# Chunked attention with a gated convolution: the first half pair in two halves, fp32 value products for part of the first group, a new order and new buffers

## Chip, cores and metric

The kernel runs on one core of a Trainium2 chip. The metric is device time in microseconds (us). Before the change the median of three runs is 286.18 us (285.96 to 287.81).

## The reference, cut to what matters

Shapes: batch 8, heads 8, sequence 576, head size 64; model width 512; chunks of 64 tokens; everything fp32.

```python
# attention inside each chunk of 64 tokens
scores = scale * np.matmul(q_c, k_c.transpose(0, 1, 2, 4, 3))      # scale = 1/8
scores = scores - np.max(scores, axis=-1, keepdims=True)
attn = np.exp(scores)
attn = attn / (np.sum(attn, axis=-1, keepdims=True) + 1e-09)
out = np.matmul(attn, v_c)
x = out.transpose(0, 2, 1, 3).reshape(B, S, 512)
# gated convolution
for k in range(5):                                                 # causal, per channel
    gate_pre += conv_w[k][None, None, :] * xp[:, k:k + S, :]
gate = 1.0 / (1.0 + np.exp(-gate_pre))
val = x @ w_val
return (gate * val @ w_out)
```

The weights arrive as 64-bit words and are turned into fp32 on the chip.

## The kernel before

**Tiling.** The 8 x 576 tokens are cut into 9 groups g of 512 tokens. In a group the heads come in two pairs of loads, p = 0 and 1 (each holds four heads of 64 channels, as two blocks of 128 channels), and the width of 512 is four blocks c or m of 128. A dense product of fp32 accuracy is made of three fp32r products: high part times high part, low weights times high x, high weights times low x; so weights and x are split into two fp32r parts.

**Pieces.** The whole program is a string of small pieces with their indices, `ORDER`; a loop at the end of the kernel (L516 on) calls one function per piece. Instructions of an engine run in the order of that string, and each engine's queue is in order. The buffers of each kind are numbered, and `SLOTS` says which number each new tile gets, in the order of the pieces; `HOME` says which kinds share buffers.

- Loads on the SyncE queue (SP): `lk`, `lq`, `lv` bring k, q, v of a pair, 512 KB each; `lw` a block of weights, 512 KB; `lc` the conv taps.
- Scores: `S g p b` is half b of a pair, 16 fp32 products of 64x64x64 on quarters of the array (32 for both halves); both halves lie in the one tile s of PSUM. `mx` (VectorE, DVE) takes the maximum, `sb` (DVE) subtracts it into an e_row buffer in SBUF, `ex` (ScalarE, ACT) takes exponentials, `sm` (DVE) sums and inverts, `nm` normalises on GpSimd (POOL) or DVE (`nmD`). Pair 0 1 has a way of its own: `mh`, `ml` split the maximum, `sp` subtracts it by four TensorE (PE) products, `ep` is the exponential from PSUM. Pairs 3 0, 4 0, 7 0, 8 0 have another: `ng`, `ea` (sixteen exponentials on ACT that also sum), `rc`.
- `T g p` transposes in eight products into the one tile et of PSUM, `ec` copies it out, `A g p` is attention times V (32 products of 64x64x64) into two PSUM tiles, u = 0 and 1.
- `xc g p u` copies x for the convolution, `xr` rounds it to its high part, `xd` makes the low part, `hl` fills the halo.
- `k0` and `k` are the conv taps, `sg` the sigmoid; `V g m c` the three value products, `vc` their eviction from PSUM to SBUF, `gs`/`gm` gate times value, `gr`, `gd` the split of that; `P g t c` the three output products, `oc` the eviction, `st` the store.
- `w1` to `w7`, `wb` turn a block of weights into fp32 (kept in `wq`) and split it into `v_hi`, `v_lo` or `o_hi`, `o_lo`.
- `W n` is n dummy bf16 products.

Products, attention times V and dummies share four PSUM buffers of one bank each, named ps. A last letter on a piece names its engine: G is GpSimd, D VectorE. All recorded instructions have the line of the helper `run`, L160, so rows are told apart by the names of their tiles (t is any buffer of the kind t2 or t4, ld any load, acc the raw weights or the conv sums).

The set `BY_HALF` is empty before; functions with an optional b work on half b of a pair when it is given.

Of the kernel before, what the change touches and what calls it, by code (L numbers as in the profile page):

```python
# [93 lines left out]

SLOTS = dict(
    ld="054321504315240135240512054310305213053400533503052304",
    ps="0000312130130213012310321023021303210321320123102031013202012013201231021301032103120302310310132013"
       "120312012032",
    acc="03210321023012302130123012",
    s="000000000000000000",  # L100
# [7 lines left out]
    mh="0",  # L108
# [12 lines left out]
def chunk_attention_gated_conv(ctx, tc, q, k, v, w_val, conv_w, w_out, out):  # L121
# [65 lines left out]
    def begin(g):  # L187
        return parts(g)[0][0]
# [383 lines left out]
```

## Time and profile before

| | |
|---|---|
| median of three runs | 286.18 us |
| profiled execution, its span | 286.4 us |
| TensorE busy | 274.4 us (96%), 3344 instructions |
| VectorE busy | 245.8 us (86%), 357 |
| ScalarE busy | 198.1 us (69%), 451 |
| GpSimd busy | 105.2 us (37%), 93 |
| DMA | 42.47 MB, mean 148 GB/s |
| chain that ended last | PE 69%, DVE 19%, DMA 3%, issue 3% |

The span goes from the first to the last instruction of the profiled execution. A busy TensorE is not TensorE at its peak: a product's record (some 0.40 us) overlaps the next one's, so prices are read as differences of starting times. Idle time of an engine that is not the bottleneck costs nothing by itself.

### The profile page before, as it was taken

The page shows a single profiled execution, that of the slowest core. Times are in us where ns is not written, and L with a number is a line of the kernel's source. Part 1 is how long each engine was busy: PE and PEld are TensorE (multiplying, and loading weights), DVE is VectorE, ACT ScalarE, POOL GpSimd, SP SyncE. Part 2 cuts the span into 40 slices and gives each one's busy share as a digit, 9 for nine tenths or more (in the row PEclk, how much of TensorE's full clock was granted, in tenths as well). Part 3 has the DMA queues.
Part 4 walks back from the last instruction along what each step waited for, and adds up shares of the span by engine and source line. Part 5 has one row for each costly group of instructions (what it writes and reads, how often), then busy time and mean ns, then how long its engine had stood idle before and what let it go on. Part 6 is the DMA issues. An engine that isn't in the chain of part 4 may idle for free.

```text
span 286.4 us, 7971 instructions
## 1 busy us (share of the span) xinstructions
PE 274.4 (96%) x3344; PEld 217.3 (76%) x3347; DVE 245.8 (86%) x357; ACT 198.1 (69%) x451; POOL 105.2 (37%) x93
## 2 busy tenths in 40 slices
PE   7978899999999999999999999989999999999994
PEld 3456688878888887878787888767678778888883
DVE  0899779999999999999999999999999899974210
ACT  2479588898999979964898696788586742751101
POOL 1457775273013506551874003976400400013100
PEclk9999799999999999999999999999999999999999
DMA  7999964457002605666250256441100121021245
GB/s 280 416 391 359 380 239 130 169 181 260 3 2 78 222 0 185 221 223 211 86 185 2 73 201 218 173 144 44 39 0 1 39 89 61 0 100 49 110 171 195
DMA packets 14291, 42.47 MB, mean 148 GB/s; under 512 B 1712, under 2 KB 1712, under 8 KB 14256
## 3 DMA queue, kind: packets, MB, share of 16 engines
q1 hardware_dynamic: 14256, 41.97, 40.9%
q8 instruction: 26, 0.43, 0.6%
q14 instruction: 9, 0.07, 0.1%
HBM read 32.53 MB, written 9.44 MB: 147 GB/s over the span
## 4 chain that ended last, share of the span: by engine, by line
PE 69%; DVE 19%; DMA 3%; issue 3%; POOL 2%; ACT 2%; SPq 0%; POOLq 0%
PE ps L160 61%; DVE acc L160 8%; PE s L160 5%; DVE t L160 4%; PE et L160 4%; DVE rs L160 3%; DMA ld<-in_v 2%; DMA ld<-in_q 1%; POOL acc L160 1%; POOL t L160 1%; DVE mx L160 1%; ACT x L160 1%; DVE t2o L160 1%; DVE t4a L160 0%; DVE x L160 0%
## 5 line engine op out<-in xcount | busy, mean ns | idle before, releaser
L160 DVE SCALAR_TENSOR_TENSOR acc<-x,cw,acc 128x516 f32<-128x516 f32 (+1 forms) x144 | 105.1, 771 | 0.9 <-POOL acc L160 0.6
L160 PE MATMUL ps<-t,v_hi 128*128 128x512 f32 x240 | 85.3, 402 | 0.0
L160 PE MATMUL ps<-t,v_lo 128*128 128x512 f32 x136 | 53.9, 396 | 0.0
L160 PEld LDWEIGHTS ps<-t,v_hi 128*128 128x128 f32 x240 | 45.2, 188 | 11.0 <-issue 0.5
L160 PE MATMUL ps<-o_hi,t 128*128 128x512 f32 x120 | 46.4, 403 | 0.8 <-ACT x L160 0.7
L160 PE MATMUL ps<-o_lo,t 128*128 128x512 f32 x76 | 30.0, 395 | 0.0
L160 DVE TENSOR_REDUCE mx<-s 128x16 f32<-128x1024 f32 x18 | 21.8, 1211 | 9.3 <-PE s L160 9.2
L160 PEld LDWEIGHTS ps<-t,v_lo 128*128 128x128 f32 x136 | 25.7, 189 | 5.1
L160 PEld LDWEIGHTS ps<-o_hi,t 128*128 128x128 f32 x120 | 22.5, 188 | 7.3 <-ACT x L160 1.1
L160 POOL TENSOR_TENSOR t<-e_row,rs 128x1024 f32<-128x1024 f32 x13 | 26.4, 2033 | 4.2 <-DVE rs L160 3.4
L160 PEld LDWEIGHTS s<-ld,ld 64*64 64x64 f32 x1152 | 19.4, 139 | 9.6 <-issue 7.7
L160 ACT CAST t<-ps 128x512 fp32r<-128x512 f32 x34 | 19.4, 596 | 10.0 <-PE ps L160 8.1
L160 PE MATMUL s<-ld,ld 64*64 64x64 f32 x1152 | 22.0, 227 | 2.9 <-issue 1.9
L160 ACT ACTIVATE e_row<-s,mx 128x64 f32<-128x64 f32 x64 | 19.0, 352 | 4.7 <-DVE mx L160 4.7
L160 POOL COPY x<-x 128x16 f32<-128x16 f32 x8 | 2.8, 354 | 52.6 <-DVE acc L160 44.9
L160 PEld LDWEIGHTS ps<-t,ld 64*64 64x64 f32 x960 | 16.3, 140 | 5.0 <-issue 2.1
L160 PE MATMUL ps<-t,ld 64*64 64x64 f32 x960 | 18.1, 225 | 1.9 <-DVE t2i L160 1.1
L160 POOL TENSOR_SCALAR acc<-x,cw 128x516 f32<-128x516 f32 (+1 forms) x7 | 12.7, 1820 | 19.2 <-ACT x L160 7.4
L160 ACT ACTIVATE acc<-x,cw 128x516 f32<-128x516 f32 (+1 forms) x24 | 17.6, 740 | 1.9 <-DVE x L160 1.8
L160 ACT ACT_TABLE_LOAD x14 | 18.0, 1283 | 0.9 <-PEq L561 0.7
L160 DVE TENSOR_REDUCE rs<-e_row 128x16 f32<-128x1040 f32 x14 | 17.2, 1228 | 1.6 <-ACT e_row L160 1.6
L160 ACT COPY x<-ps 128x512 f32<-128x512 f32 (+3 forms) x38 | 16.0, 476 | 3.3 <-issue 2.0
(302 smaller groups left out, 572.5 us busy)
## 6 DMA issues: line engine op xcount, KB each, us to landing
ld<-in_k SPq DMA_DIRECT2D x18, 512.0 KB, 5.8
ld<-in_q SPq DMA_DIRECT2D x18, 512.0 KB, 5.9
ld<-in_v SPq DMA_DIRECT2D x18, 512.0 KB, 5.0
out<-t SPq DMA_DIRECT2D x10, 256.0 KB, 2.3
acc<-in_moe_w_val SPq DMA_DIRECT2D x4, 512.0 KB, 7.5
acc<-in_moe_w_out SPq DMA_DIRECT2D x4, 512.0 KB, 7.1
out<-t2j SPq DMA_DIRECT2D x3, 256.0 KB, 2.5
out<-t2b SPq DMA_DIRECT2D x3, 256.0 KB, 3.1
```

What stands on the lines that cost most here:

```text
L160: return tc.keep_in_program_order(fn(*args, **kwargs))
```

## The change

**What it does.** Pair 0 0 is worked in halves: each half of its scores has a PSUM tile of its own (s and et), and `mx`, `sb`, `ex`, `sm`, `nm`, `T`, `ec` and `A` are called for each half, while the loads stay whole. In group 0, for channel blocks c = 0 and 1 (pair 0), a new piece `F g m c` makes the value product as one fp32 product from the fp32 weights in `wq` and the x of the convolution; the eight products of `F` stand for 24 of `V`, and `xr 0 0`, `xd 0 0` are gone. The order of all pieces and all buffer numbers are new, with some pieces on other engines. `ea` is written as four calls of `ey`, with the same sixteen exponentials.

```diff
-ORDER = """zw,lk 0 0,zi,lq 0 0,W 8,lw v 2,lw v 0,lq 0 1,zr 1,zm,lk 0 1,lw v 1,zr 0,lv 0 0,lq 1 0,S 0 0 0,S 0 0 1,W 15,mx 0 0,
+ORDER = """zw,zi,zr 0,zr 1,lk 0 0,lq 0 0,W 2,zm,W 1,W 2,lw v 3,lw v 2,w1G v 2,w5 v 2,S 0 0 0,lw v 0,mx 0 0 0,sb 0 0 0,S 0 0 1,
...
-BY_HALF = set()
+BY_HALF = {(0, 0)}
...
     def sc(g, p, b):
-        if b == 0:
-            s_ps[g, p] = tile_of("s", [P, 2, 2, 4, D], F32, banks)
-        at = s_ps[g, p]
-        if b == 1 and (g, p) in BY_HALF:
-            at = s_ps[g, p, 1] = tile_of("et", [P, 2, 2, 4, D], F32, banks)
+        alone = (g, p) in BY_HALF
+        if b == 0 or alone:
+            s_ps[g, p, b] = tile_of("et" if b else "s", [P, 2, 2, 4, D], F32, banks)
+        at = s_ps[g, p, b if alone else 0]
...
-    def sm(g, p):
+    def sm(g, p, b=None):
-        rss[g, p] = r = tile_of("rs", [P, 16], F32)
-        run(V.tensor_reduce, out=r, in_=probs[g, p], op=ALU.add, axis=AX.X)
+        if (g, p) not in rss:
+            rss[g, p] = tile_of("rs", [P, 16], F32)
+        r, e = rss[g, p], probs[g, p]
+        if b is not None:
+            r, e = r.rearrange("p (h b c) -> p h b c", h=2, b=2)[:, :, b], half_rows(e, b)
+        run(V.tensor_reduce, out=r, in_=e, op=ALU.add, axis=AX.X)
         run(V.reciprocal, out=r, in_=r)
...
-    def tr(g, p):
-        et_ps[g, p] = tile_of("et", [P, 8, P], F32, banks)
+    def tr(g, p, b=None):
+        if (g, p) not in et_ps:
+            et_ps[g, p] = tile_of("et", [P, 8, P], F32, banks)
         for j in range(8):
-            run(E.transpose, out=et_ps[g, p][:, j, :], in_=normed[g, p][:, 2 * j:2 * j + 2, :].rearrange("p b k -> p (b k)"), identity=ident)
+            if b is not None and j // 2 % 2 != b:
+                continue
+            at = j if b is None else 4 * b + 2 * (j // 4) + j % 2
+            run(E.transpose, out=et_ps[g, p][:, at, :], in_=normed[g, p][:, 2 * j:2 * j + 2, :].rearrange("p b k -> p (b k)"), identity=ident)
...
+    def vf(g, m, c):
+        if c == 0:
+            v_ps[g, m] = tile_of("ps", [P, T], F32, banks)
+        run(E.matmul, v_ps[g, m], lhsT=wq["v", c].bitcast(F32)[:, m * P:(m + 1) * P], rhs=xs[g][:, c, begin(g):],
+            start=c == 0, stop=c == NH - 1)
...
-                  S=sc, mx=mx, sb=sb, ex=ex, sm=sm, ng=ng, ea=ea, rc=rc, nm=nm, T=tr, ec=ec, A=av, hl=hl, xc=xc, xr=xr, xd=xd, k0=k0,
+                  S=sc, mx=mx, sb=sb, ex=ex, sm=sm, ng=ng, ea=ea, ey=ey, rc=rc, nm=nm, T=tr, ec=ec, A=av, hl=hl, xc=xc, xr=xr, xd=xd, k0=k0,
```

**What moves, on TensorE.** The first value products of group 0. Before, on TensorE, the transposes of pair 0 1 (et_356) and the score piece of pair 1 1 (s_369) stand ahead of the first group of three fp32r products (t_348 is the rounded x, t4a its low part):

```order
L160 MATMUL et_356<-ident,t_339 128x128 x8
L160 MATMUL s_369<-ld_161,ld_226 64x64 x32
L160 MATMUL ps_410<-t_348,v_hi 128x512
L160 MATMUL ps_410<-t_348,v_lo 128x512
L160 MATMUL ps_410<-t4a,v_hi 128x512
```

After, the score piece of pair 1 0 is followed by single products of x_224 (the x of the convolution) with t_154 and t_246 (the fp32 weights of blocks 0 and 1), and transposes stand between them:

```order
L160 MATMUL s_312<-ld_307,ld_309 64x64 x32
L160 MATMUL ps_351<-x_224,t_154 128x512
L160 MATMUL et_358<-ident,t_356 128x128 x8
L160 MATMUL ps_351<-x_224,t_246 128x512
L160 MATMUL ps_393<-x_224,t_154 128x512
```

One product of x and a weight block now stands where three stood, and the casts of x are not ahead of it.

**What moves, on ScalarE, in the start.** Before, from the split of the maximum of pair 0 1 (mh) to the first copies of x (e_row_65<-s is `ep`, t4b<-et is `ec 0 0`, t_348<-ps is `xr 0 0`):

```order
L160 CAST mh_236<-mx_228 128x16
L160 ACTIVATE t2n<-acc_99 128x512
L160 ACTIVATE t2o<-t2o 128x512
L160 ACTIVATE e_row_65<-s_183 128x16x64
L160 COPY t4b<-et_250 128x1024
L160 CAST v_hi<-t2q 128x512
L160 CAST t_348<-ps_300 128x2x256
L160 COPY x_163<-ps_301 128x2x256
L160 CAST t_348<-ps_301 128x2x256
```

After, from the same mh to the second copy of x (ps_255 and ps_256 are the results of `A 0 0`):

```order
L160 CAST mh_217<-mx_215 128x16
L160 CAST v_hi<-t_154 128x512
L160 COPY t_234<-et_226 128x2x256 x2
L160 ACTIVATE t_244<-t_244 128x512
L160 ACTIVATE e_row_65<-s_179 128x16x64
L160 CAST v_hi<-t_231 128x512
L160 CAST v_hi<-t_246 128x512
L160 COPY x_224<-ps_255 128x2x256
L160 ACTIVATE t2a<-acc_242 128x512
L160 COPY x_224<-ps_256 128x2x256
```

Three roundings of weights (v_hi) stand there where one stood, the copies of the two halves of `ec 0 0` (t_234) come ahead of `ep` and not behind it, and the two casts of x are gone.

**What moves, on ScalarE, ahead of the first sixteen exponentials.** Before, between the copy `ec 1 1` and the group `ea 3 0` (the last row):

```order
L160 COPY t_726<-et_707 128x1024
L160 ACTIVATE e_row_65<-e_row_65 128x16x64
L160 ACTIVATE t2b<-t2b 128x512
L160 CAST t_821<-ps_771 128x2x256
L160 COPY t2j<-ps_666 128x512
L160 CAST t_821<-ps_772 128x2x256
L160 COPY x_618<-ps_772 128x2x256
L160 COPY x_618<-ps_771 128x2x64
L160 COPY x_618<-ps_771 128x2x192
L160 COPY t2d<-ps_700 128x512
L160 COPY t_857<-et_812 128x1024
L160 ACTIVATE e_row_64,rs_871<-s_734,mx_837 128x64 x16
```

After, from the exponential `ex 2 1` to the same group:

```order
L160 ACTIVATE e_row_65<-e_row_65 128x16x64
L160 COPY t2q<-ps_351 128x512
L160 COPY x_514<-ps_768 128x2x64
L160 COPY x_514<-ps_768 128x2x192
L160 CAST t_817<-ps_769 128x2x256
L160 COPY x_514<-ps_769 128x2x256
L160 CAST t_817<-ps_768 128x2x256
L160 ACTIVATE t2o<-t2o 128x512
L160 ACTIVATE acc_840<-x_514,cw 128x516
L160 ACTIVATE acc_842<-x_514,cw 128x516
L160 COPY t_862<-et_804 128x1024
L160 ACTIVATE e_row_64,rs_900<-s_733,mx_834 128x64 x16
```

One eviction of value products (t2q) stands there where two stood (t2j, t2d), two conv starts (acc) stand between the casts of x and the last copy of transposes, and the group follows that copy in both.

## Rows read from the trace of the kernel before

**Rows 1.** Table of stages; columns as in its first line, counts in parentheses.

```profile
core 0: us, PE busy (x) PEld busy (x) DVE busy (x) ACT busy (x) POOL busy (x), PEclk, DMA share, GB/s
...
23.10:34.69 11.59, 9.62 (x225) 7.20 (x215) 10.39 (x17) 8.28 (x16) 7.71 (x6) 0.85 0.99 364
...
62.00:136.00 74.00, 73.17 (x986) 59.75 (x985) 71.82 (x106) 63.16 (x136) 27.00 (x21) 1.00 0.43 146
136.00:204.00 68.00, 66.14 (x894) 53.10 (x893) 66.51 (x90) 55.57 (x128) 36.66 (x28) 1.00 0.36 119
...
sum 286.40, PE 274.43 PEld 217.33 DVE 245.78 ACT 198.05 POOL 105.18; mean PE 30.49 PEld 24.15 DVE 27.31 ACT 22.01 POOL 11.69
```

**Rows 2.** Timeline of PE: start, duration, tiles, count; waits and their releasers in brackets.

```profile
64.68 1.16 PE L160 MATMUL ps<-t,ld 64*64 64x64 f32 x64 [0.83 <-DMA ld<-in_v]
...
190.06 1.16 PE L160 MATMUL ps<-t,ld 64*64 64x64 f32 x62 [1.07 <-DVE t2i L160]
...
203.97 0.50 PE L160 MATMUL ps<-o_hi,t 128*128 128x512 f32 x1 [0.67 <-ACT x L160]
```

**Rows 3.** Table of stages, columns as in rows 1, the stretch at a lower clock.

```profile
31.06:34.47 3.41, 3.41 (x63) 2.55 (x65) 3.41 (x6) 0.81 (x2) 1.66 (x2) 0.50 1.01 359
```

**Rows 4.** Timeline of PE: score pieces and the first value product.

```profile
12.29 1.16 PE L160 MATMUL s<-ld,ld 64*64 64x64 f32 x64
...
23.18 0.50 PE L160 MATMUL ps<-t,v_hi 128*128 128x512 f32 x1
...
29.76 0.81 PE L160 MATMUL s<-ld,ld 64*64 64x64 f32 x40 [1.94 <-issue]
```

**Rows 5.** Timeline of PE without pauses: score, attention times V, transposes.

```profile
37.67 1.16 PE L160 MATMUL s<-ld,ld 64*64 64x64 f32 x64
38.76 0.50 PE L160 MATMUL ps<-t,v_hi 128*128 128x512 f32 x1
...
45.70 1.11 PE L160 MATMUL ps<-t,ld 64*64 64x64 f32 x64
46.74 1.10 PE L160 MATMUL et<-ident,t 128*128 128x128 f32 x8
47.59 0.48 PE L160 MATMUL ps<-t,v_hi 128*128 128x512 f32 x1
```

**Rows 6.** Timeline of PE: the last five products, first and last.

```profile
281.46 0.40 PE L160 MATMUL ps<-o_lo,t2a 128*128 128x512 f32 x1
...
282.39 0.39 PE L160 MATMUL ps<-o_hi,t2h 128*128 128x512 f32 x1
```

**Rows 7.** Timeline of POOL: the third and the fourth load arrive.

```profile
7.18 0.63 POOL L160 TENSOR_SCALAR t<-acc 128x512 f32<-128x512 f32 x1 [5.79 <-DMA acc<-in_moe_w_val]
...
8.52 0.64 POOL L160 TENSOR_SCALAR t2s<-acc 128x512 f32<-128x512 f32 x1 [0.65 <-DMA acc<-in_moe_w_val]
```

**Rows 8.** Groups by line and form, 5 to 45 us: busy, mean ns.

```profile
L160 DVE TENSOR_REDUCE mx<-s 128x16 f32<-128x1024 f32 x6 | 7.3, 1214 | 9.3 <-PE s L160 9.2
...
L160 ACT COPY x<-ps 128x512 f32<-128x512 f32 x5 | 2.8, 590 | 0.0
...
L160 ACT ACTIVATE e_row<-s 128x1024 f32<-128x1024 f32 x1 | 1.0, 1026 | 0.1
...
L160 DVE TENSOR_TENSOR t4b<-ps,t 128x512 fp32r<-128x512 f32 x2 | 1.3, 674 | 0.0
...
L160 DVE SCALAR_TENSOR_TENSOR t2r<-t,t2r 128x512 uint32<-128x512 uint32 x1 | 0.7, 683 | 0.0
```

**Rows 9.** Timeline of ACT: first exponential of ea 3 0, eviction after it.

```profile
51.81 0.32 ACT L160 ACTIVATE e_row<-s,mx 128x64 f32<-128x64 f32 x1 [0.93 <-DVE mx L160]
...
56.57 0.67 ACT L160 COPY t2i<-ps 128x512 f32<-128x512 f32 x1
```

**Rows 10.** Table of stages, columns as in rows 1, ten microseconds of the middle.

```profile
80.00:90.00 10.00, 10.00 (x107) 8.10 (x106) 9.93 (x18) 9.97 (x40) 0.54 (x1) 1.00 0.01 2
```

**Rows 11.** Groups by line and form, whole span: a DVE step beside POOL.

```profile
L160 DVE TENSOR_TENSOR t2o<-t,t2n 128x512 fp32r<-128x512 f32 x1 | 2.1, 2135 | 0.0
```

More of the change, by code (lines that the diff above doesn't have):

```diff
@@ L293, in mx @@
         if b is None:
-            run(V.tensor_reduce, out=mxs[g, p], in_=flat(s_ps[g, p]), op=ALU.max, axis=AX.X)
+            run(V.tensor_reduce, out=mxs[g, p], in_=flat(s_ps[g, p, 0]), op=ALU.max, axis=AX.X)
         else:
@@ L302, in sb @@
         if b is None:
-            run(V.tensor_tensor, out=e, in0=flat(s_ps[g, p]), in1=wide(mxs[g, p]), op=ALU.subtract)
+            run(V.tensor_tensor, out=e, in0=flat(s_ps[g, p, 0]), in1=wide(mxs[g, p]), op=ALU.subtract)
         else:
@@ L353, in rc, with ey @@
-    def rc(g, p):
+    def ey(g, p, i):
+        if (g, p) not in probs:
+            probs[g, p] = e_rows[next(e_slot)]
+            rss[g, p] = tile_of("rs", [P, 16], F32)
+        h, b = i // 2, i % 2
+        at = half_scores(g, p, b)
+        for c in range(4):
+            j = 4 * i + c
+            run(S.activation, out=probs[g, p][:, j, 0:D], in_=at[:, h, c], func=AF.Exp, bias=mxs[g, p][:, j:j + 1],
+                scale=SCALE, accum_out=rss[g, p][:, j:j + 1])
+    def ea(g, p):
+        for i in range(4):
+            ey(g, p, i)
@@ L367, in ec, with nm @@
-    def ec(g, p, copy=S.copy):
-        probs_t[g, p] = tile_of("eb", [P, 2, 2, 2, P], F32)
-        run(copy, out=probs_t[g, p].rearrange("p h b a q -> p (h b a) q"), in_=et_ps[g, p])
-    def av(g, p):
+    def nm(g, p, *half):
+        *b, on = half if half and not isinstance(half[-1], int) else (*half, G)
+        if (g, p) not in normed:
+            normed[g, p] = tile_of("en", [P, 16, D], F32)
+        out, e, r = normed[g, p], probs[g, p][:, :, 0:D], wide(rss[g, p])
+        if b:
+            out, e = half_rows(out, *b), half_rows(e, *b)
+            r = rss[g, p].rearrange("p (h b c) -> p h b c", h=2, b=2)[:, :, b[0]].unsqueeze(3).broadcast_to([P, 2, 4, D])
+        run(on.tensor_tensor, out=out, in0=e, in1=r, op=ALU.mult)
@@ L373, in av @@
+    def av(g, p, only=None):
         et, vv = probs_t[g, p], vt[g, p]
         for u in range(2):
-            x_ps[g, p, u] = tile_of("ps", [P, 2, 2, 2, D], F32, banks)
-        for b in range(2):
+            if (g, p, u) not in x_ps:
+                x_ps[g, p, u] = tile_of("ps", [P, 2, 2, 2, D], F32, banks)
+        for b in range(2) if only is None else [only]:
             for a in range(2):
@@ L399, in xc @@
             if lo < hi:
-                run(copy, out=xs[g][:, 2 * p:2 * p + 2, col + lo - t:col + hi - t],
+                run(copy, out=x_of(g)[:, 2 * p:2 * p + 2, col + lo - t:col + hi - t],
                     in_=x_ps[g, p, u].rearrange("p b a w t -> p b (a w t)")[:, :, lo - u * half:hi - u * half])
@@ L406, in xr @@
     def xr(g, p, u):
-        if u == 0:
+        if (g, p) not in xh:
             xh[g, p] = tile_of("xh", [P, 2, T], F32R)
```

227 lines of the change are left out of this document (119 added, 108 removed).

## The prediction

> **What bounds the kernel now.** I read the table of stages first. TensorE (PE) is the engine to beat: between 62 and 136 us it is busy for 73.17 of 74.00 us, between 136 and 204 us for 66.14 of 68.00 [rows 1]. So from about 35 us on only two things move the end: the amount of TensorE work, and its few stalls. Three of them exceed 0.6 us: one attention-times-V piece waits 0.83 us for its V load, one waits 1.07 us for a copy on VectorE (DVE), one output product waits 0.67 us behind ScalarE (ACT); together 2.6 us [rows 2]. The start is another matter. Between 23.10 and 34.69 us TensorE has pauses and a mean granted clock of 0.85 [rows 1], and within that, from 31.06 to 34.47, the clock is 0.50, that is 1.2 GHz and not 2.4 [rows 3]; the pause ahead of it, in which the second half of a score piece waited, ends at 29.76 [rows 4].
>
> The loss of the start can be counted. The unit prices of TensorE at full clock are differences of starting times: a score piece S 1.09 us (37.67 to 38.76), an attention-times-V piece A 1.04 (45.70 to 46.74), a transpose piece T 0.85 (46.74 to 47.59) [rows 5]; one fp32r 128x512 product 0.2325 (281.46 to 282.39 in four steps) [rows 6]. The four products that subtract the maximum (sp) I set at 4 x 0.2325, 0.9. By 34.69 us the kernel has done 5 S, 3 T, 3 A, sp and 12 value products: 5.45 + 2.55 + 3.12 + 0.9 + 2.79 = 14.8 us of work. So 19.9 us are lost by then. After the last product's start at 282.39 [rows 6] come 4.0 us of copy and store.
>
> **The first part: half pair and loads.** TensorE's first scores are no bottleneck by themselves: what they do is wait for loads. Usable 512 KB loads come 1.34 us apart (GpSimd, POOL, meets the third at 7.18, the fourth at 8.52) [rows 7]. Pair 0 1, which every later step needs, is complete with the seventh load now, not the sixth: 8.52 + 3 x 1.34 = 12.5 us. Before, it began at 12.29 [rows 4], for dummy products stood ahead of it. So the halves of pair 0 0 gain little on the way to the first value product; they let max, subtraction and exponential of one half lie beside the load of the other.
> From 12.5 I walk the queues: S 1.09, maximum 1.21 [rows 8], to 14.8. On DVE two weight steps stand ahead of the small split ml (0.68 for one of two SBUF operands [rows 8]; the other, of one operand, I set at 0.5): to 16.0. ml 0.1 and sp 0.9: 17.0. ACT has a rounding, two half copies and a conversion ahead of ep since 14.8, some 2.3 us, and is there in time. The exponential ep 1.03: 18.1. Behind it ACT has two roundings of weights, one conversion and two copies of x; the copy's 0.59 [rows 8] for each of the five, as all are 128x512 steps: 3.0, and some 0.2 for the hand-over. The first F product of the new kind starts at 21.3; the first value product before was at 23.18 [rows 4].
>
> **F instead of three products.** 24 products of 0.2325 (5.6 us) become 8 of fp32. No row has an fp32 128x512 product. Below, it cannot be cheaper than one fp32r product, 0.2325, which gives 1.9 us in all, a gain of 3.7. Above, its multiply-adds are as many as those of one S piece (32 fp32 products of 64x64x64), which uses the array in quarters and takes 1.09 [rows 5]: 8.7, a loss of 3.1. The S piece is the nearest row, being fp32 too, so I stay near it, with 0.9: 7.2 us, 1.6 us more TensorE work.
> The Trainium skill ("FP8 and Floating Point Precision", section "TensorE Precision Notes") says that true FP32 takes four passes through the array. By that one F would be an estimated 0.93 us, and the sum 0.2 us higher; no run here shows it yet.
> What F takes away are two casts and two splits of x (2 x 0.59 on ACT, 2 x 0.68 on DVE [rows 8]); F waits for the plain copies only.
>
> **The end of the start.** From 21.3 TensorE's own work up to the end of A 1 0 is 8 F, 2 T, 2 A, 3 S and 15 products: 7.2 + 1.7 + 2.1 + 3.3 + 3.5 = 17.8. My walk finds two waits in it: 1.2 us where the third product of group 0, block 2 needs xd 0 1 1, which stands on DVE behind sum, reciprocal and weight steps; and 0.6 us at S 2 0, which needs the one score buffer that the subtraction of 1 1 still reads. That makes 40.9. Done by then are 6 S, 3 T, 3 A, sp, and the worth of 24 + 15 products: 6.54 + 2.55 + 3.12 + 0.9 + 9.07 = 22.2. Lost: 18.7, against 19.9. The start gains 1.2 us, the price of F being in it. No pause of my walk is as long as the one before 29.76, so I put no half clock into it.
>
> **The middle.** All of the rest is a new order and new buffers. The three stalls above (2.6 us) are each a matter of one neighbour in the queue, and in the new order none of the three has the same neighbour; I count them as gone. What is late next: S 3 1 needs the score buffer that the sixteen exponentials ea 3 0 read. Before, such a group lasted from 51.81 to 56.57, 4.8 us [rows 9]. In the new order ACT has, between A 1 0 and ea 3 0, eight copies or casts of x, two evictions, one exponential, two copies of transposes (about 1 us each) and two conv starts, some 11 to 12 us: ea starts at 52 to 53, ends at 57 to 58. TensorE's work up to S 3 1 is 51 products, S, A and 2 T: 11.9 + 1.1 + 1.0 + 1.7 = 15.7, to 56.6. A stall between 0.4 and 1.4; I take 1.0.
> By the order of the program, 21 tensor-tensor steps leave DVE, most for POOL, and 12 evictions, 7 copies of x and 2 copies of transposes leave it, most for ACT. At 0.68 a step [rows 8] and 1.2 for each of the larger two that is 14.3 + 12.9 + 2.4 = some 30 us of DVE's 245.78 [rows 1]; ACT gains about 12 evictions and 5 copies of x at 0.59, 10 us, on its 198.05. The loads keep their number, 101 transfers issued in all; their order changes. All this is hidden as long as the helpers are ahead of TensorE, and the cover is thin in one place: between 80 and 90 us ACT is busy for 9.97 of 10.00, DVE for 9.93 [rows 10]. I cost it at nothing; if ACT is late by its full 10 us, most of that would show.
> One rule speaks against the move. In the row, a DVE product of two SBUF operands took 2.14 us once [rows 11], where a step of that kind takes 0.68 [rows 8]. The Trainium skill ("SBUF — State Buffer", section "Who interferes with whom") says that a DVE instruction with two SBUF inputs contends with a GpSimd instruction reading SBUF. The trace agrees in that row.
> If each of the twenty moved steps lengthened one such DVE step by 1.45 us, DVE would get its 29 us back and nothing would be freed; that is the second rival below.
> The tail has the same shape (four products, eviction, store): 4.0 us, no change.
>
> **Sum.** 286.4 - 1.2 (start) - 2.6 (stalls gone) + 1.0 (S 3 1) = 283.6. The profiled execution was 0.2 us above the median of 286.18; so 283.4.
>
> **Rivals.**
> 1. The gain is larger: the two waits of the walk (1.8 us) close because DVE is freed, and the stall at S 3 1 (1.0) does not come. 283.4 - 2.8 = 280.6; with F at 0.8 too, 279.8. For it: DVE is the busiest helper and loses the most. Against: the walk has DVE's relief in it already.
> 2. The change does not do what it says beyond the start: the stalls are replaced by others of the same size, because DVE's relief is eaten by POOL or because single buffers decide. 286.2 - 1.2 + 1.0 = 286.0; from 285 to 288. For it: ACT and DVE are both full from 80 to 90 us.
> 3. Slower: ACT's queue. Evictions that now stand on ACT wait behind each of the four groups of sixteen exponentials (4.8 us). TensorE needs the product buffer (four banks) and stops. If 2 us are lost at each, 8 us: 283.4 + 8 = 291.4; it decides (over 289.0) from 1.4 us each. For it: a store of products behind a 4.8 us block. Against: before, an eviction stood right behind a group as well (56.57 [rows 9]) and TensorE did not stop there.
> 4. Slower: the clock. There are 24 dummy products and not 31, five and not eight before the first scores. Each stretch like that of 31.06 to 34.47 at half clock costs 1.7 us [rows 3]; four of them give 290.2, and it decides past three. Against: the pauses of my walk are shorter.
>
> **Chances.** The forecast 0.38, own range 281.5 to 285.5; rival 1 0.25; rival 2 0.17; rival 3 0.12; rival 4 0.08. One per cent, about what a measurement of this kernel tells from no change, puts the bounds at 283.3 and 289.0. The forecast lies on the first of them: 0.18 of its 0.38 is faster, 0.20 same. Faster 0.25 + 0.18 = 0.43, same 0.20 + 0.17 = 0.37, slower 0.20. The range takes in rival 1 with F at 0.7 (279) and rival 3 at its turning point (290); left out are most of rivals 3 and 4 and F near its lower bound.
>
> **What would show it.** In the profile after: the first F at 21 to 22 us, eight F records or pairs of them at about 0.9 us pitch; A 1 0 ending near 41; no slice of PEclk under 9 after 13 us; the three stalls gone; a wait of about 1 us at S 3 1 near 57, released by ACT; DVE busy about 216 us, ACT about 208, POOL well above its 105. I am wrong if F starts past 23, if TensorE waits for ACT in several places between 50 and 200, or if a stretch at 0.50 appears.

## The result and the profile after

The changed kernel takes 288.65 us (median of seven runs, 287.86 to 289.11), the one before 286.0 beside it (285.01 to 287.81). The ratio is 1.0085, with a 95% interval from 1.0061 to 1.0109: slower by 0.9%, where 283.4 us, 0.9% less, was forecast, and inside the range given, 279 to 290. The profiled execution has a span of 286.5 us and took 288.26 us of device time: what lies around the span is 1.8 us. The ratios and their intervals here and below leave out executions more than 1.5% above the fastest of their kernel; the medians take in all.

Table of stages of the changed kernel (columns as in [rows 1]):

```profile
21.76:40.20 18.44, 18.34 (x364) 12.24 (x367) 18.18 (x27) 14.56 (x24) 12.97 (x12) 1.00 0.89 332
40.20:54.00 13.80, 10.35 (x185) 8.23 (x176) 13.63 (x16) 9.77 (x18) 12.56 (x7) 1.00 0.65 230
...
62.00:136.00 74.00, 73.11 (x959) 59.50 (x957) 73.37 (x104) 63.55 (x137) 37.84 (x28) 1.00 0.38 130
136.00:204.00 68.00, 67.73 (x965) 55.58 (x964) 66.20 (x84) 57.20 (x131) 34.40 (x28) 1.00 0.44 144
...
sum 284.00, PE 271.19 PEld 214.00 DVE 240.34 ACT 207.50 POOL 145.97; mean PE 38.74 PEld 30.57 DVE 34.33 ACT 29.64 POOL 20.85
```

Between 40.2 and 54 us TensorE is busy for 10.35 of 13.80 us: 3.45 us are lost in this one stretch. Between 62 and 136 us the loss is about that of before (0.89 against 0.83), between 136 and 204 it is 0.27 against 1.86 [rows 1]. VectorE is busy for 240.34 us, not for some 216; ScalarE (207.50) came out as forecast, and GpSimd is at 145.97.

TensorE's timeline (start, duration, tiles, count, wait before it):

```profile
21.76 1.12 PE L160 MATMUL ps<-x,t 128*128 128x512 f32 x2 [0.46 <-ACT x L160]
...
23.59 1.88 PE L160 MATMUL ps<-x,t 128*128 128x512 f32 x4
25.41 1.16 PE L160 MATMUL ps<-t,ld 64*64 64x64 f32 x64
...
39.07 1.37 PE L160 MATMUL ps<-t,ld 64*64 64x64 f32 x64
42.13 1.09 PE L160 MATMUL et<-ident,t 128*128 128x128 f32 x8 [1.69 <-POOL t L160]
...
53.16 0.50 PE L160 MATMUL ps<-t,v_hi 128*128 128x512 f32 x1 [1.60 <-DVE t L160]
...
94.93 1.28 PE L160 MATMUL ps<-t,ld 64*64 64x64 f32 x64 [0.78 <-ACT x L160]
```

The first F starts at 21.76 us (forecast 21.3), before the first value product of [rows 4]; two F (four records) take 1.82 us, from 23.59 to 25.41. A 1 0 starts at 39.07 and its last record ends at 40.44, before the forecast 40.9. The three waits of [rows 2] are gone. In their stead TensorE waits 1.69 us at the transposes T 1 1 for a GpSimd step, 1.60 us at a value product for VectorE, 0.78 us at A 3 0.

What VectorE did ahead of two of these waits (taps are acc<-x,cw,acc; t2r is the weight step w3 o 1):

```profile
31.99 2.72 DVE L160 SCALAR_TENSOR_TENSOR acc<-x,cw,acc 128x512 f32<-128x512 f32 x2
...
37.09 1.50 DVE L160 SCALAR_TENSOR_TENSOR acc<-x,cw,acc 128x512 f32<-128x512 f32 x1
...
50.38 2.13 DVE L160 TENSOR_SCALAR t2r<-acc 128x512 uint32<-128x512 uint32 x1
```

and what GpSimd did meanwhile (a weight sum, two low parts of weights, the normalisations of 1 1 and 2 1):

```profile
31.00 1.28 POOL L160 TENSOR_TENSOR t2e<-t2e,t2h 128x512 uint32<-128x512 uint32 x1 [1.05 <-DVE cw L160]
...
32.89 1.28 POOL L160 TENSOR_TENSOR v_lo<-t,v_hi 128x512 fp32r<-128x512 f32 x1
...
36.74 1.30 POOL L160 TENSOR_TENSOR v_lo<-t,v_hi 128x512 fp32r<-128x512 f32 x1
40.17 1.90 POOL L160 TENSOR_TENSOR t<-e_row,rs 128x1024 f32<-128x1024 f32 x1 [2.13 <-DVE rs L160]
...
50.06 2.17 POOL L160 TENSOR_TENSOR t<-e_row,rs 128x1024 f32<-128x1024 f32 x1 [0.77 <-ACT t2o L160]
```

Two taps take 2.72 us (0.84 and 1.85 by their own records, which overlap a little), one 1.50, and a weight step 2.13, next to GpSimd steps of 1.28 to 2.17 us in the same time. The normalisation of 1 1, for which the transposes wait, itself waited 2.13 us for the sum on VectorE. With GpSimd idle a tap takes 0.746 us in this trace: 89 of the 144 taps run clear of GpSimd, with that mean, and the other 55 take 1.19 us; before, 32 ran beside it, at 0.87 (I counted a tap as clear where GpSimd was busy for less than 5% of it). The groups by form say the same of the total, 126.5 us:

```profile
L160 DVE SCALAR_TENSOR_TENSOR acc<-x,cw,acc 128x516 f32<-128x516 f32 x112 | 94.8, 885 | 0.6
L160 DVE SCALAR_TENSOR_TENSOR acc<-x,cw,acc 128x512 f32<-128x512 f32 x32 | 31.7, 1017 | 0.5 <-ACT acc L160 0.3
```

against the 105.4 of before:

```profile
L160 DVE SCALAR_TENSOR_TENSOR acc<-x,cw,acc 128x516 f32<-128x516 f32 x112 | 81.9, 774 | 0.7 <-POOL acc L160 0.6
L160 DVE SCALAR_TENSOR_TENSOR acc<-x,cw,acc 128x512 f32<-128x512 f32 x32 | 23.5, 759 | 0.2
```

So there are two questions: from what did the waits between 40 and 54 us come, VectorE's order or its drawn-out steps; and what do F and the halves bring for themselves?

### The profile page after: what moved, and what is told of

It is laid out like the page before. It is cut to its first block, busy times and chain, and to the rows that moved or that the text cites. A ratio compares the mean times of both kernels' runs of the same rounds, so it can differ in the third digit from the quotient of the medians.

```text
span 286.5 us, 7934 instructions
## 1 busy us (share of the span) xinstructions
PE 271.2 (95%) x3332; PEld 214.0 (75%) x3332; DVE 240.3 (84%) x320; ACT 207.5 (72%) x469; POOL 146.0 (51%) x115
## 4 chain that ended last, share of the span: by engine, by line
PE 53%; DVE 36%; ACT 4%; DMA 3%; issue 2%; SPq 1%; DVEq 0%; ACTq 0%
PE ps L160 48%; DVE acc L160 18%; DVE t L160 5%; DVE rs L160 4%; DVE mx L160 4%; PE et L160 3%; DMA acc<-in_moe_w_val 3%; PE s L160 2%; DVE e_row L160 1%; ACT t L160 1%; DVE t2r L160 1%; DVE t2p L160 1%; ACT e_row L160 1%; SPq L160 1%; ACT x L160 1%
## 5 line engine op out<-in xcount | busy, mean ns | idle before, releaser
L160 DVE SCALAR_TENSOR_TENSOR acc<-x,cw,acc 128x516 f32<-128x516 f32 (+1 forms) x144 | 125.9, 915 | 1.1 <-ACT acc L160 0.3
L160 PE MATMUL ps<-t,v_hi 128*128 128x512 f32 x224 | 78.9, 404 | 2.0 <-DVE t L160 1.8
L160 PE MATMUL ps<-t,v_lo 128*128 128x512 f32 x104 | 41.0, 394 | 0.0
L160 POOL TENSOR_TENSOR t<-e_row,rs 128x1024 f32<-128x1024 f32 (+1 forms) x14 | 27.4, 1963 | 23.9 <-DVE rs L160 13.6
L160 DVE TENSOR_REDUCE mx<-s 128x16 f32<-128x1024 f32 (+1 forms) x18 | 21.2, 1179 | 5.5 <-PE s L160 5.5
L160 PE MATMUL ps<-o_lo,t 128*128 128x512 f32 x60 | 23.6, 394 | 0.0
L160 PEld LDWEIGHTS ps<-t,v_lo 128*128 128x128 f32 x104 | 19.6, 188 | 4.6 <-issue 0.7
L160 PE MATMUL et<-ident,t 128*128 128x128 f32 x128 | 17.6, 279 | 3.1 <-POOL t L160 1.7
L160 DVE TENSOR_TENSOR t<-ps,t 128x512 fp32r<-128x512 f32 x26 | 17.1, 681 | 3.6 <-ACT t L160 3.6
L160 ACT ACTIVATE t<-acc 128x512 f32<-128x512 f32 (+8 forms) x31 | 13.2, 471 | 8.8 <-DMA acc<-in_moe_w_val 6.3
L160 PE MATMUL ps<-t,ld 64*64 64x64 f32 x960 | 17.8, 221 | 0.9 <-ACT x L160 0.8
```

The lines of the kernel that those rows point to most:

```text
L160: return tc.keep_in_program_order(fn(*args, **kwargs))
```

## Experiments

Each time is a median, and each ratio is to the kernel before, run beside it; that one came out between 285.81 and 286.26 us, so differences of less than some 0.5 us between runs are not read. Pieces of the order are named as in the program. "Changed" is the kernel with the change, 288.65 us.

**The kernel before, once more.**

> The kernel before, unchanged, for a second profile. Theory A (the profiled execution on which the prediction was summed was a long one: its 286.4 us span carries a 2.16 us pause at 27.6 us and a half-clock stretch of 3.41 us, while the other runs' device time of 286.0 holds some 1.8 us outside the span): the span of this profile is near 284.2 us, without the half-clock stretch. Rival B (the profile was typical): span near 286.4 again, clock 0.50 from about 31 us. Ratio 1.000 in both.

285.89 us beside 285.81, ratio 1.0015. Its profiled execution was again a long one, span 287.0 us, 288.81 us of time, with the pause and the half clock:

```profile
27.50:30.50 3.00, 0.56 (x25) 0.42 (x24) 2.33 (x6) 2.81 (x7) 2.05 (x2) 1.00 0.96 358
...
32.30:35.30 3.00, 3.00 (x67) 2.21 (x66) 2.98 (x6) 0.00 (x0) 0.79 (x1) 0.50 0.97 333
```

The spans and mean clocks of the other executions tell that most are not like this. Of 120 runs of the kernel before that stood beside the experiments, 105 had a mean clock of 0.997 or more, with a median span of 284.1 us; 15 had 0.992 to 0.994, 11 of them with a span of 286 us or more, as only 4 of the 105 had. Device time minus span is some 1.8 us in each. Theory A holds, though not by its profile: the execution on which the prediction was summed was some 2.2 us longer than the usual one.

**VectorE's queue in another order.**

```diff
-sb 1 1, k 0 0 1, k 0 0 2, ... mx 2 0, sb 2 0, ... k 0 3 1, ... sm 1 1, sm 2 0
+sb 1 1, mx 2 0, sb 2 0, ... sm 1 1, sm 2 0, k 0 0 1, k 0 0 2, k 0 3 1
```

> The changed kernel, but three conv taps of group 0 (k 0 0 1, k 0 0 2, k 0 3 1) stand on VectorE behind the sums of pairs 1 1 and 2 0, not ahead of them. Theory A (the order of VectorE's queue delays the sum of 1 1, and with it normalisation and the transposes T 1 0/T 1 1, which waited 1.69 us at 42.1): the wait goes, 1 to 1.7 us less than the changed kernel, 287.0 to 287.6. Rival B (something later, the V product that waited 1.60 us at 53.2 for VectorE, takes it all back): 288.4 to 288.8, with that wait grown to about 3 us.

289.02 us. The wait at the transposes is gone, but the three taps now run beside the normalisations, at 1.54 us in the mean on VectorE (1.30, 2.28 and 1.09):

```profile
39.13 4.62 DVE L160 SCALAR_TENSOR_TENSOR acc<-x,cw,acc 128x512 f32<-128x512 f32 x3
```

and the score piece behind them waits on TensorE for the score buffer:

```profile
46.33 1.16 PE L160 MATMUL s<-ld,ld 64*64 64x64 f32 x64 [2.58 <-issue]
```

The subtraction of 2 1, which reads that buffer, stands on VectorE behind the taps and ends at 46.23. The wait at the V product near 54 is as long as it was, 1.58. The order moves the wait: nearer rival B, 0.2 above its total and at another place than it named.

**The weight step alone.**

```diff
-w1 o 1, w3 o 3, ... sm 2 1, k 0 1 1, w3 o 1, ... xd 1 1 1
+w1 o 1, w3 o 1, w3 o 3, ... sm 2 1, k 0 1 1, ... xd 1 1 1
```

> The changed kernel, but the weight step w3 of block o 1, which took 2.13 us on VectorE at 50.38 beside GpSimd's normalisation of pair 2 1, stands right behind w1 of that block, some 5 us earlier. Theory A (that one step makes the low part of x late for the V product that waited 1.60 us at 53.2): the wait falls below 0.3 us and the time by 1 to 1.6 us, 287.0 to 287.6. Rival B (VectorE is behind by more than this step, so the wait only moves): less than 0.5 us gained.

287.26 us, 1.4 less, as theory A had it. The wait near 53 is gone, one of 0.97 us at 49.7 takes its place: w3 o 1 takes 0.82 us there and w3 o 3, behind it, 1.50 beside other GpSimd steps, ahead of a split of x.

**GpSimd's steps later, VectorE's order kept.**

```diff
-wb v 3, ... k 0 3 1, w1G o 3, k0G 0 1, wb v 1, ... nm 1 1, nm 2 0
+wb v 3, ... k 0 3 1, ... nm 1 1, nm 2 0, w1G o 3, k0G 0 1, wb v 1
```

> The changed kernel, but three GpSimd steps between 34 and 38 us (w1 of weight block o 3, the conv start k0 0 1, the low part of weight block v 1) stand behind the normalisation of pairs 1 1 and 2 0. VectorE's own order is that of the changed kernel. Theory A (conv taps on VectorE take 1.36 to 1.50 us and not 0.75 beside GpSimd reading SBUF, and this makes the sum of 1 1 late): the two later taps fall to 0.75, the sum of 1 1 starts 1.2 to 1.4 us earlier, the wait of 1.69 us at the transposes falls to 0.3 to 0.5. Rival B (only the order on VectorE counts): taps as long, wait 1.7. Total between 287.2 and 288.6, as the moved steps press later.

288.1 us. The tap at 37.8, now with GpSimd idle, takes 0.74 and not 1.50; the pair ahead of it, still beside a weight sum and a low part, 2.73. The wait at the transposes falls from 1.69 to 0.93, not to theory A's 0.3 to 0.5, and the delayed GpSimd steps make waits of 1.24 and 0.40 us at 64, behind which the clock is 0.50 from 65.1 to 68.5 us in the profiled execution. Contention is there, but postponed it is paid elsewhere.

**GpSimd steps that only write.** Here VectorE's order is untouched, and six, then nine GpSimd steps are memsets.

```diff
-wb v 3, wb v 1, k0G 0 1, w2G o 3, wb o 0, k0G 0 2
+memsets of the same tiles on GpSimd
```

> The changed kernel, order and VectorE's own steps untouched, but six GpSimd steps between 31 and 55 us that read SBUF (two low parts of weights of v, one of o, two conv starts, one weight scaling) are memsets of the same outputs, which only write; the three normalisations there stay. The output leaves out these six steps. Theory A (VectorE is drawn out by GpSimd steps that read SBUF beside it): the two taps at 32.0, 1.36 us each, and the one at 37.1, 1.50, fall to 0.75; the weight step of 2.13 us stays long, since it runs beside a normalisation; the wait at the transposes near 40 to 42 us falls from 1.69 to below 0.9 us; 287.0 to 288.0. Rival B (VectorE's order alone): taps as long or the wait unchanged at 1.5 to 1.9, 288.3 to 289.

285.44 us, 3.2 less than the changed kernel and more than theory A asked for. On VectorE, the two taps, the third, and the weight step w3 o 1:

```profile
32.05 1.63 DVE L160 SCALAR_TENSOR_TENSOR acc<-x,cw,acc 128x512 f32<-128x512 f32 x2
...
36.05 0.74 DVE L160 SCALAR_TENSOR_TENSOR acc<-x,cw,acc 128x512 f32<-128x512 f32 x1
...
47.34 2.13 DVE L160 TENSOR_SCALAR t2r<-acc 128x512 uint32<-128x512 uint32 x1
```

On GpSimd, a memset beside the second of the two taps, the normalisation for which the transposes wait, and the one beside that weight step:

```profile
32.92 0.52 POOL L160 MEMSET v_lo<- 128x512 f32 x1
...
38.38 1.90 POOL L160 TENSOR_TENSOR t<-e_row,rs 128x1024 f32<-128x1024 f32 x1 [3.21 <-DVE rs L160]
...
47.02 2.17 POOL L160 TENSOR_TENSOR t<-e_row,rs 128x1024 f32<-128x1024 f32 x1 [3.47 <-DVE rs L160]
```

The taps fall from 2.72 to 1.63 for two, and from 1.50 to 0.74 (GpSimd is idle beside the third now); the weight step beside the normalisation stays at 2.13. The wait at the transposes is gone, the one near 50 us is 0.78. That memsets are shorter on GpSimd itself does not explain this: in both kernels GpSimd stood idle ahead of that normalisation, waiting for VectorE's sum (2.13 and 3.21 us), and the sum is what came earlier. The gain arises where the two waits were: S 3 0 (45.23 us in the changed kernel) starts 1.79 us earlier, S 3 1 (60.31) 3.04 earlier, and every later score piece 3.0 to 3.1.

```diff
-nm 1 1, nm 2 0, nm 2 1
+memsets of the same tiles on GpSimd, beside the six above
```

> As the run before, with the three normalisations (1 1, 2 0, 2 1) as memsets too, so that GpSimd reads no large tile of SBUF from 31 to 55 us; the transposes no longer wait for the sums there, either. The output leaves out the nine steps. Theory A: the weight step w3 o 1 falls from 2.13 to 0.42 us, the wait of 1.60 us at the V product near 53 falls below 0.3, and both waits together (3.3 us) are gone: 284.9 to 286.0. Rival B (VectorE is too late without contention as well): the wait near 53 stays above 1 us, 286.8 or more.

282.74 us (three of the four executions took 282.39 to 282.94), 5.9 less than the changed kernel and 0.987 of the one before (0.982 to 0.993). The third tap, now beside a memset, and the same weight step on VectorE:

```profile
36.08 0.74 DVE L160 SCALAR_TENSOR_TENSOR acc<-x,cw,acc 128x512 f32<-128x512 f32 x1
...
47.14 0.42 DVE L160 TENSOR_SCALAR t2r<-acc 128x512 uint32<-128x512 uint32 x1
```

and the memset on GpSimd:

```profile
35.89 0.96 POOL L160 MEMSET t4b<- 128x1024 f32 x1
```

The tap takes 0.74, the weight step 0.42, and TensorE has no wait between 40 and 56 us. That stretch here,

```profile
40.00:56.00 16.00, 16.00 (x223) 13.30 (x215) 15.93 (x26) 15.34 (x52) 1.58 (x1) 1.00 0.56 200
```

and in the changed kernel:

```profile
40.00:56.00 16.00, 12.55 (x207) 10.08 (x199) 15.83 (x21) 10.93 (x25) 12.77 (x7) 1.00 0.56 198
```

VectorE is as full as ever (15.93 of 16.00), but it gets through, and TensorE gains 3.45 us. The wait of 0.78 at A 3 0 near 94 is gone as well, though nothing was changed there. Theory A, with more than it asked for: S 3 1 starts 4.1 us earlier than in the changed kernel, the score pieces from 109 us on 5.7. Memsets wait for no input, and the normalisations are then no longer behind the sums; so the second run shows contention and this shorter path together; the first shows contention without it, as far as the transposes go.

**The same move in the kernel before.**

```diff
-gs and gdD of groups 0 to 4 on VectorE (20 steps)
+gsG and gd on GpSimd
```

> The kernel before with nothing changed but twenty tensor-tensor steps (gate times value and its low part, groups 0 to 4) moved from VectorE to GpSimd. Without contention VectorE would lose 20 x 0.68 = 13.6 us. Theory A (conv taps and steps with two SBUF operands run longer beside GpSimd): VectorE falls by less than 8 us, taps beside GpSimd are at 1.0 us or more in the mean, and the time does not fall: 285.8 to 288. Rival B (the work is hidden): VectorE falls by 12 to 14 us, taps as before, 284.5 to 286.

294.25 us, ratio 1.027: slower than theory A's 288 as well, though on its side of the question. Busy times and the taps:

```profile
PE 275.1 (94%) x3347; PEld 216.8 (74%) x3347; DVE 248.6 (85%) x337; ACT 197.9 (67%) x451; POOL 133.5 (45%) x113
```

```profile
L159 DVE SCALAR_TENSOR_TENSOR acc<-x,cw,acc 128x516 f32<-128x516 f32 x112 | 92.6, 871 | 4.5 <-POOL acc L159 2.7 <-ACT acc L159 1.7
```

Twenty steps were taken from VectorE, 13.6 us by their price, and it became busier, 248.6 us and not 245.8; 112 taps take 92.6 us, not 81.9. Of its 144 taps, 48 run beside GpSimd, at 1.05 us. TensorE now waits 2.6 us in all for ScalarE's roundings behind those steps and 1.7 for GpSimd's low parts themselves. VectorE's growth is the mechanism by itself, without the new order. The lost time is not: a step of the moved kind takes some 1.4 us on GpSimd and not 0.7, and TensorE waits for it directly. How much of the 8 us is which was not separated.

**More repairs of the order.** Three further kernels moved VectorE's pieces so that the waits of the changed kernel should vanish.

> The changed kernel with three repairs: the sum of pair 1 1 stands ahead of a maximum and two conv taps and its normalisation ahead of three GpSimd steps; the normalisation of 2 1 is on VectorE, so that the weight step w3 o 1 no longer runs beside GpSimd; the taps k 1 0 4 and k 2 0 1 stand behind the splits of x of 3 0. Theory A (three VectorE delays beside GpSimd make the waits of 1.69, 1.60 and 0.78 us of TensorE): all three fall below 0.4 us, 3.0 to 4.0 us less, 284.6 to 285.7. Rival B (they move on): more than half comes back, above 287.

290.1 us, rival B: the third repair put two taps beside a gate product and a normalisation of GpSimd, where they took 3.38 us, and A 3 0 waited 1.75 us, with a clock of 0.62 from 96 to 100 us. Of the other two waits 0.98 us is left, near 49, and 0.96 in two pieces comes at 64.

```profile
91.55 3.38 DVE L160 SCALAR_TENSOR_TENSOR acc<-x,cw,acc 128x516 f32<-128x516 f32 x2
```

> The run with three repairs without its third one (the taps of group 1 stand where the changed kernel has them). Theory A (the first two repairs work and the third cost the loss, as its two taps took 3.38 us beside GpSimd and held up an eviction on VectorE): no wait over 1.3 us at 94, 286.0 to 287.3. Rival B (the first two repairs press later): 288 or more.

287.75 us, between both theories: the transposes no longer wait; 0.98 us at 48.5, 0.98 in two pieces at 64 and 0.82 at 94 stay.

> The changed kernel with VectorE relieved between 31 and 54 us: three taps of block 0 of group 0 stand just ahead of its fourth, near 60 us, one tap of block 3 behind the subtraction of 2 1, one behind a split of x, and the weight step w3 o 1 early, as in the run that had only that. Theory A (VectorE, drawn out beside GpSimd, makes TensorE's waits of 1.69 and 1.60 us): both fall below 0.4, 285.2 to 286.4. Rival B (the taps press elsewhere before 80 us): waits of as much at 57 to 80 us, 287 to 289.

288.64 us, rival B: no wait over 0.3 us from 40 to 60 us, and then one of 2.10 for VectorE:

```profile
64.26 1.16 PE L160 MATMUL ps<-t,ld 64*64 64x64 f32 x62 [2.10 <-DVE t L160]
```

Behind it the clock is 0.50 from 65.72 to 69.14 us, which takes back some 1.7 us more.

**F undone.**

```diff
-F 0 0 0, sm 0 1, nmD 0 1, T 0 1, ... (eight F)
+xr 0 0 0, xr 0 0 1, xd 0 0 0, xd 0 0 1, V 0 0 0, sm 0 1, nmD 0 1, T 0 1, ... (V for F, wb v 1 earlier)
```

> The changed kernel with its eight F products undone: 24 fp32r value products, with the two casts of x on ScalarE and the two splits on VectorE ahead of the first of them. TensorE's work falls by 8 x (0.91 - 0.70) = 1.7 us. Theory A (F costs more on TensorE than its missing casts and splits save): 287.0 to 288.0, faster than the changed kernel by 0.7 to 1.7. Rival B (the first product waits longer for splits of x and weights, and VectorE, late already, is later by 1.3 us): 288.6 to 290, the pause before the first value product grows to 2 us or more.

293.76 us, above both forecasts: with the splits ahead of the sum of 0 1 the transposes waited 2.83 us, and the clock is 0.50 from 25.83 to 32.66 us, half of which, some 3.4 us, is lost as well.

```profile
27.27 1.97 PE L160 MATMUL et<-ident,t 128*128 128x128 f32 x8 [2.83 <-DVE t L160]
```

> The eight F products undone once more, but with the splits of x of pair 0 0 behind the normalisation of pair 0 1 on VectorE and the transposes of 0 1 ahead of the first value product, so that those do not wait for the splits. Theory A (the 5.1 us that the first undoing cost came from where the splits stood): the pause of 3.33 us at the transposes falls below 1 us, 288 to 290. Rival B (VectorE has no room for the splits in this order at all): over 291.5.

289.78 us. With the splits behind the normalisation that wait falls to 0.70, and waits of 0.34, 0.92 and 0.87 us for low parts and casts follow before 32 us; no stretch at half clock is in its profile. So F costs 8 x (0.91 - 0.70) = 1.7 us of TensorE and saves more, some 1 us net, in this order, which was made for it.

**The halves undone.**

> The changed kernel with pair 0 0 whole again: one maximum, one subtraction, one sum, one set of transposes. Theory A (halves gain nothing, since pair 0 1, complete with the seventh load at 12.5 us, sets the start): the same within 0.5 us of 288.65, first F still at 21.5 to 22. Rival B (halves bring the first F forward): first F later by 1 us or more, 289.5 to 290.5.

288.51 us beside 288.65: halves change nothing that can be measured in the whole. The first F comes at 22.27 us for 21.76, a little later than theory A allowed.

**The three waits of the kernel before.**

```diff
-... lv 3 1 ... A 2 0, lv 2 1 ... sm 7 1, vc 6 1, hl 7, gd 4 0, V 5 1 2, vcD 6 2 ... sm 8 1 ... xd 7 1 1
+... lv 2 1 ... A 2 0, lv 3 1 ... vc 6 1, hl 7, gd 4 0, V 5 1 2, vcD 6 2, sm 7 1 ... xd 7 1 1, sm 8 1, nm 8 1
```

> The kernel before with only the three waits of TensorE over 0.6 us in its middle aimed at: the V load of pair 2 1 takes the place and buffer of the load of 3 1; the sum of 7 1 stands behind the eviction for which A 7 0 waited; the sum of 8 1 and its normalisation stand behind the splits of x of 7 1. Theory A (each wait is a matter of one neighbour in a queue, as the prediction had it): all three fall below 0.3 us, 2.0 to 2.6 us less than before, 283.4 to 284.2. Rival B (VectorE is full there, and the delay only moves): less than 1 us gained, with new waits of the same size within 10 us behind each place.

287.77 us beside 286.13, ratio 1.0034 (0.9995 to 1.0074). The wait for V is gone; the two others come back behind their places, with 0.98 and 1.90 us:

```profile
192.09 1.09 PE L159 MATMUL et<-ident,t 128*128 128x128 f32 x8 [0.98 <-POOL t L159]
...
214.28 0.59 PE L159 MATMUL ps<-o_hi,t 128*128 128x512 f32 x1 [1.90 <-DVE t2a L159]
```

Behind the second the clock is 0.50 for 3.4 us. Rival B: with VectorE full, a delay taken from one step is the next one's.

**Complete kernels with GpSimd relieved.**

```diff
-k0G 0 1, k0G 0 2, k0G 1 1, w2G o 3, ... w3 o 1 behind k 0 1 1
+k0 0 1, k0 0 2, k0 1 1, w2 o 3 (ScalarE), ... w3 o 1 behind w1 o 1
```

> The changed kernel, complete, with GpSimd relieved between 34 and 54 us by giving work to ScalarE, which waits for VectorE there: three conv starts (0 1, 0 2, 1 1) and one weight scaling (o 3) on ScalarE, and w3 o 1 early. Theory A (less reading by GpSimd lets VectorE through, and ScalarE has room): 285.5 to 286.8, the tap at 37 us at 0.75. Rival B (ScalarE becomes late): new waits of TensorE for ScalarE between 40 and 70 us, 287.5 or more.

285.97 us, 2.7 less than the changed kernel, level with the one before (ratio 0.9992, 0.9970 to 1.0015). On VectorE the two taps, the third and w3 o 1:

```profile
31.95 2.74 DVE L160 SCALAR_TENSOR_TENSOR acc<-x,cw,acc 128x512 f32<-128x512 f32 x2
...
37.06 0.74 DVE L160 SCALAR_TENSOR_TENSOR acc<-x,cw,acc 128x512 f32<-128x512 f32 x1
...
45.05 0.42 DVE L160 TENSOR_SCALAR t2r<-acc 128x512 uint32<-128x512 uint32 x1
```

The third tap is at 0.74, since the low part that stood beside it comes earlier on GpSimd and has ended, and the weight step is at 0.42; the first two still run beside GpSimd. Of the 2.7 us, the weight step's move brought 1.4 by itself (above). One wait is left before 60 us, at the transposes:

```profile
41.34 1.09 PE L160 MATMUL et<-ident,t 128*128 128x128 f32 x8 [0.93 <-POOL t L160]
```

> As the run beside it (without the conv start 1 1), and the sum of 1 1 ahead of a maximum, its normalisation ahead of three GpSimd steps, one tap behind the subtraction of 2 0 and one behind a split of x. Theory A: the waits at 40 and at 48 to 53 us all fall below 0.5 us, 284.5 to 286. Rival B (VectorE has no room, they press later): 287 or more.

286.49 us: with the sum moved as well, A 1 1 waits 0.87 us for ScalarE and A 3 0 0.75; no gain.

> The kernel of the run e14 (conv starts and a weight scaling on ScalarE, w3 o 1 early), with one more GpSimd step (w7 of block o 0) out of the way of two taps, and the sum of 1 1 straight behind the subtraction of 2 0. Theory A (the rest of the wait at 40 us, 0.93, is contention at 32 to 35 us and the sum's place): the wait falls below 0.3 us and the pair of taps at 32 us from 2.74 to 2.1 or less; 284.7 to 285.4. Rival B: it presses later, 285.8 or more.

285.53 us, ratio 0.9976 (0.9947 to 1.0005): the wait at the transposes is gone, and one of 1.57 us at S 2 0 stands at 32, since a weight step now runs beside GpSimd for 1.73 us. No complete kernel was found that is faster than both beyond its interval; this one is the nearest.

## Why the prediction was wrong

**What held.** The first F came at 21.76 us for 21.3, A 1 0 ended at 40.44 for 40.9, so the walk of the start was 0.5 us too long: its two waits of 1.8 us did not come (TensorE is busy for 18.34 of 18.44 us from 21.76 on), and the work of 17.8 took some 0.9 more. F costs 0.91 us for 0.9: the choice near the S piece held. That is 3.9 times the 0.2325 of an fp32r product. The Trainium skill ("FP8 and Floating Point Precision", section "TensorE Precision Notes") gives four passes for true FP32; the estimate of 0.93 from that agrees. The three waits of [rows 2] are gone. ScalarE is busy 207.5 us for 208. No stretch at half clock appeared (the clock of rival 4), and the queue of ScalarE behind the exponentials (rival 3) did not stop TensorE. So none of the signs for which it said "I am wrong if" came; of what it asked to see, VectorE's 216 us (240 came) and the wait at S 3 1 were missing.

**The step that failed: "I cost it at nothing".** The prediction let VectorE lose 30 us by moving its steps, most to GpSimd, priced each at the 0.68 of a clear row, and put no price on what stays on VectorE beside them. It had the row of 2.14 us [rows 11] and the rule before it, and turned both into a rival of 286 us, with a chance of 0.17. VectorE lost 5.4 us. The taps alone took back 21 of the 30 (126.5 against 105.4), the eight steps w3 2.6 (5.8 against 3.2), and six weight steps w1 that came over from GpSimd, which the prediction did not count, another 2.6. The price stood in the trace of the kernel before, and more than "once": beside the 2.14 two more steps of that kind took 1.80 and 1.61 us, and 32 taps ran beside GpSimd, the longest for 1.81 us. Three runs bear on the cause. With the order kept and six of GpSimd's reading steps made writes, the taps there take 0.74 to 0.82 and 3.2 us come back; this is the plainest. With the normalisations as well it is 5.9, part of it by a shorter path. With the order of before kept and twenty steps moved, VectorE grows where it should have shrunk. What the delays cost the changed kernel is the 3.45 us between 40 and 54, the sum's largest missing term. The Trainium skill ("SBUF — State Buffer", section "Who interferes with whom") has the rule, that an instruction with two SBUF inputs contends with a GpSimd instruction that reads SBUF and not with one that only writes it. The trace agrees with it here: a tap takes 0.746 us clear of GpSimd, 1.19 in the mean beside it, and 0.74 beside a memset.

**The execution on which the sum was made.** "The profiled execution was 0.2 us above the median" compared a span with a device time. The two differ by 1.8 us, so the execution of 286.4 took some 288.2 (an estimate), 2.2 above the median of 286.0, with the half clock that most executions don't have. The sum of 283.6 is a span and means 285.4 us of time: 0.2% under the kernel before, no gain to be measured, even if each of its terms had held. The "19.9 us lost" of the start and the gain of 1.2 against it are those of this execution.

**The wait at S 3 1** (1.0 us) did not come, and that was luck, for both sides of it were late. Timelines of ACT (first and last record of the sixteen exponentials) and of PE (first half of S 3 1):

```profile
55.01 0.31 ACT L160 ACTIVATE e_row<-s,mx 128x64 f32<-128x64 f32 x1 [0.84 <-DVE mx L160]
...
59.56 0.30 ACT L160 ACTIVATION_READ_ACCUMULATOR e_row<-s,mx 128x1 f32 x1
```

```profile
60.31 0.69 PE L160 MATMUL s<-ld,ld 64*64 64x64 f32 x32
```

The exponentials began at 55.01 us, not at 52 to 53, as ScalarE waited 1.90 and 0.84 us for VectorE ahead of them; TensorE, held up between 40 and 54 us, came at 60.31, not at 56.6. In the run with nine memsets, which held up neither, they began at 50.23 and TensorE came at 56.19, again without a wait: the walk of ScalarE was over 2 us too long.

**The stalls "are each a matter of one neighbour".** They went with the new order, but removing their neighbours in the old one (the run above) moved two of three. The gain of 2.6 is real in the new order, less the new 0.78 at A 3 0.

Together, in spans: 283.6 forecast; -0.5 for the start, +3.45 for the waits at 40 to 54, -1.0 for S 3 1, +0.8 for A 3 0 make 286.35; measured 286.5. In time 1.8 more, and 0.4 for the median over the profiled execution (288.65 against 288.26).

**Open.** Why some executions of the kernel before pause for 2 us at the score piece near 28 us, after which the clock is 0.50, wasn't found; the profile shows nothing for which TensorE waits there. In each of the eight profiled executions with a stretch at 0.50 in its middle, that stretch begins in or soon behind a wait of TensorE of more than 1 us; but the waits of 1.69 and 1.60 us in the changed kernel had none behind them. How much of the 5.9 us of the last memset run is the shorter path and not contention was not separated either.

## What to carry to other kernels

Before moving a step from VectorE to GpSimd, look at what VectorE does at that time: in these traces a step of two SBUF operands that began beside a tensor-tensor step of GpSimd did not end before that one had ended (a tap of 0.746 us took up to 2.40), and the engine that was to be relieved may end up busier. Give such a step to ScalarE where it has room, or put it beside VectorE's PSUM reads. And sum a forecast on an execution that stands for the others: compare span with span and time with time, and look whether a pause or a lower clock in its profile is in the other runs too.

## What the runs showed of the hardware

A tap that began beside a running tensor-tensor step of GpSimd (a gate product, a low part, a normalisation), with 0.2 us of it or more to come, ended 0.55 us after that step's end: all 28 of them in the changed kernel, 6 in the kernel before and 15 in the run with twenty moved steps, between 0.544 and 0.557 us, whether the tap took 0.75 us or 2.40. So what it loses goes by what is left of the other step, and is not a share of its speed. One of the 28, with the step beside it:

```profile
191.89 2.14 POOL L160 TENSOR_TENSOR t<-t2d,t2r 128x512 f32<-128x512 f32 x1 [0.85 <-ACT t2r L160]
```

```profile
192.80 1.78 DVE L160 SCALAR_TENSOR_TENSOR acc<-x,cw,acc 128x516 f32<-128x516 f32 x1
```

Beside the conv starts of GpSimd, which read one tensor, nine taps of the changed kernel took 0.66 to 1.18 us, and five of them ended before that step did; beside a memset a tap took 0.74.

A VectorE step of one SBUF operand, the uint32 w3, took 0.42 us alone and 2.13 beside a normalisation of 2.17 us on GpSimd; it ended 0.28 us after the normalisation, in the changed kernel and with six memsets alike. VectorE's reads of PSUM (maximum 1.21, subtraction 1.22, split of x 0.68 us in the mean) were the same beside GpSimd and without it.
